# Routed experts behind a gated attention: where the first expert's weight steps stand, in which order two layers load, and where the last ranking stands

## The chip, the cores and the metric

The kernel runs on one core of a Trainium2 chip. The metric is the device time of one execution in microseconds; 0.5% of it is about 5 us. PE is the matmul engine (TensorE), ACT ScalarE, DVE VectorE, POOL GpSimd, SP the engine that issues most loads. [...]

## What is computed

```python
for t in range(S):                       # gated attention, 4 x 8 heads, 768 steps, head size 48
    state = alpha[:, :, t, :, None] * state + einsum('bhd,bhe->bhde', k[:, :, t], v[:, :, t])
    y[:, :, t] = einsum('bhd,bhde->bhe', q[:, :, t], state)
x = y as (3072, 384)
x = ((x @ w1) * (x @ w2)) @ w3 @ w_out   # dense gated layer, inner width 1024
logits = x @ w_gate + log1p(exp(x @ w_noise)) * noise      # 8 experts
top2, weights = the two largest of each token, their softmax
for e in range(8):                       # routed experts, 384 -> 1024 -> 384
    h = maximum(x[mask] @ ew1[e], 0)
    out[mask] += weight[mask] * (h @ ew2[e])
```

## The kernel before

**Three stages.** The attention and the dense layer are interleaved by a planner (L1150 to L1190): PE's order is written out by the program, the other engines' order is made by a scheduler when the kernel is built. Tokens go in eight groups g of 384. A group's dense layer is 16 wide units (`wide`, L523: for each of eight slices f and two matrices i, nine matmuls of 384 columns; ACT takes the result out as ab, DVE multiplies the two, L540, and splits the product into gh and gl, L181 and L183) and six narrow units (`narrow`, L546: twelve matmuls of 400 columns; three tiles t, two parts each). With the last narrow unit `finish` (L566) and `route` (L604) follow: some fifty small steps on DVE that end with the sums over R and the counts M (L645 to L648).

**Ranking.** `rank(g)` (L651) adds up the counts by two small matmuls (L657, L658), works out each token's row on DVE (L660 to L683, the rows are ad) and writes six lots into a table in device memory from POOL (L686). Group g-1 is ranked amid group g's wide units, behind slice RF in the last group. The first expert's part 0 needs the ranking of groups 0 to 6: SP then loads its slots mt from the table (L946), POOL gathers the tokens' rows xg (L887), and PE turns them (`turn_part`, L895) between the last narrow units. The last group's ranking, `rank(NG - 1)`, is called in `experts` among the first expert's tiles.

**An expert.** Part 0 has 512 slots, part 1 has 320. Layer 1 is eight units (`first`, L972, nine matmuls each: L902 to L904), whose result ACT splits off as hh (L905) and DVE as hl (L906). Layer 2 is a tile of 24 matmuls (`second`, L912 to L914), scaled by the factors wv (L951, from mt and the two scales) into ysb and added to the output by an indirect write from POOL (L936). Expert 0 and expert 1 are opened together: part 0 of expert 0, part 0 of expert 1, then the two parts 1.

**Weight steps.** Each layer's weights are loaded in halves into es (three tiles, L855), then cut into eh and el. `weight_steps` (L842) lists the steps: two loads, two maxima over a half (L858; the second also writes em, L861), an empty step, a small matmul of em on PE (`over_all`, L866), the scales on DVE (L870 to L874), then the cuts (ACT writes eh, L181, DVE writes el, L185). They wait in the list `todo`, and `prepare(n)` (L1014) takes n of them, each set behind the last DVE and ACT instruction of the program so far. A load takes a free es tile, so the fourth load waits for the cuts of the first half. In the list, layer 1's steps stand ahead of layer 2's. Before the change the first expert's steps begin behind the last group's ranking of group 6, one after each further wide and narrow unit (`prepare_after`); `leave(n)` in `experts` takes steps until n are left.

Of the kernel before, what the change touches and what calls it, by code (L numbers as in the profile page):

```python
# [24 lines left out]
E = 8  # L25
NK = DM // P
# [4 lines left out]
NG = NTOK // G  # L31
# [7 lines left out]
EST = P * TCOLS  # L39
NTA = G0 // P  # L40
NFR = 2
RF = 3
RG = 6
PA = 1
WB = 12
# [12 lines left out]
Q2 = 3  # L58
Q3 = 1
Q4 = 1  # L60
ST1 = 13
ST2 = 11
T0 = 1
T1 = 2
PGL = range(4)
NPC = 4
PB = 512
# [18 lines left out]
def body(ctx, tc, q, k, v, alpha, mw1, mw2, mw3, mwo, wg, wn, noise, ew1, ew2, out, dbg=None):  # L86
# [710 lines left out]
    def mix_units():  # L797
        fu = fuse_units()
        for g in range(NG):
            for f in range(NF):  # L800
                for i in range(2):
                    if g == 0:
                        yield (0.0, (lambda f=f: convert((f // 4 + 1) * 2 * NK + AH)), TG - 1)
                    yield (1.48, (lambda g=g, f=f, i=i: wide(g, f, i)), (g + 1) * TG - 1)
                    if g == NG - 1 and f > RF:
                        yield (0.0, (lambda: prepare_after(LAST[-1], PA)), 0)
                    if g == 0 and f >= FF:
                        c, x, n = next(fu)
                        yield 0.0, (lambda n=n: convert(n + AH)), 0
                        yield c, x, 0  # L810
                if f == (RF if g == NG - 1 else RG) and g:
                    yield (0.1, (lambda g=g: LAST.append(rank(g - 1))), 0)
                    if g == NG - 1:
                        yield (0.0, begin_experts, 0)
            if g == 0:
                for c, x, n in fu:
                    yield 0.0, (lambda n=n: convert(n + AH)), 0
                    yield c, x, 0
                yield (0.0, end_of_weights, 0)
            for t in range(TG):  # L820
                for part in range(2):
                    yield (2.05, (lambda g=g, t=t, part=part: narrow(g, t, part)), 0)
                    if g == NG - 1:
                        yield (0.0, (lambda: prepare_after(LAST[-1], PA)), 0)
                        if 0 <= t * 2 + part - T0 < NTP[0]:
                            yield (0.34, (lambda i=t * 2 + part - T0: turn_part(0, 0, i)), 0)

# [3 lines left out]
    def expert_weights(e):  # L831

        r, steps = [], []
        for j, (src, n, m) in enumerate(((ew1, NK, F), (ew2, NF, DM))):
            sc = ep.tile([P, 8], F32, name=f"esc{j}")
            hi = ep.tile([P, n, m], F16, name=f"eh{j}")
            lo = ep.tile([P, n, m], F16, name=f"el{j}")
            r += [hi, lo, sc]
            steps += weight_steps(src, e, n, m, hi, lo, sc)
        return r, steps  # L840

    def weight_steps(src, e, n, m, hi, lo, sc):  # L842

# [89 lines left out]
    def put(py, n, mt, wv, t, e=None):  # L933
        ys = ep.tile([P, DM], F32, name="ysb", bufs=3)
        nc.scalar.activation(ys[:n], py, AF.Copy, scale=wv[:n, t:t + 1])  # L935
        i = nc.gpsimd.indirect_dma_start(  # L936
            out=out, out_offset=bass.IndirectOffsetOnAxis(ap=mt[:n, t, 0:1].bitcast(U32), axis=0),
            in_=ys[:n], in_offset=None, compute_op=OP.add)
        if e == E - 1:
            for o in adds.setdefault(e, []):  # L940
                tc.declare_no_dep(i.ins, o.ins, reason="an expert has each token once")
            adds[e].append(i)
# [17 lines left out]
    def fetch_part(e, p):  # L960
        c0, c1 = PARTS[p]
        t0, nt = c0 // P, -(-(c1 - c0) // P)
        rows = P + NTOK - (G if e < NFR and p == 0 else 0)
        mt = slots(table[e, :, t0:t0 + nt, :], nt, p)
        xT = ep.tile([P, 2 * NK, nt * P], F16, name=f"xT{p}", bufs=1)
        EX[e, p] = (mt, xT, [gather(mt, t, rows) for t in range(nt)])
# [30 lines left out]

        return rest

    def begin_experts():  # L1000
        nonlocal ep
        ep = ctx.enter_context(tc.tile_pool(name="ep", bufs=2, side="right", reuse_waits="tile"))
        weights_for(0)
        fetch_part(0, 0)

    def weights_for(e):
        EW[e], st = expert_weights(e)
        todo.extend(st)

    def prepare_after(ins, n):  # L1010
        with tc.issue_after(ins):
            prepare(n)

    def prepare(n):  # L1014

        if not n or not todo:
            return
        with ExitStack() as st:
            for e in (mybir.EngineType.DVE, mybir.EngineType.Activation):
                for i in [i for i in nc.cur_bb.bb.instructions[-60:] if i.engine == e][-1:]:  # L1020
                    st.enter_context(tc.issue_after(i))
            for _ in range(min(n, len(todo))):
                todo.pop(0)()
# [4 lines left out]
    def experts():  # L1028
        leave(ST2)
        weights_for(1)  # L1030
        fetch_part(1, 0)
        for f in range(NF):
            first(0, 0, f)
            prepare(Q1)
        leave(ST1 + ST2)
        for t in range(NTP[0]):
            turn_part(1, 0, t)
            second(0, 0, t)
            prepare(Q2)
            if t == 1:  # L1040
                rank(NG - 1)
        fetch_part(0, 1)
        fetch_part(1, 1)
        leave(ST2)
        for f in range(NF):
            first(1, 0, f)
            prepare(Q3)
            if 0 <= f - NF + NTP[1] + T1 < NTP[1]:
                turn_part(0, 1, f - NF + NTP[1] + T1)
        for f in range(NF):  # L1050
            first(0, 1, f)
            prepare(Q4)
        leave(0)
        weights_for(2)
        for t in range(NTP[1] - 1):
            turn_part(1, 1, t)
            second(0, 1, t)
            prepare(2)
        turn_part(1, 1, NTP[1] - 1)
        rest = last_few(0)  # L1060
        prepare(2)
        li = overflow_plan()
        for e in range(1, E):
            if 1 < e < E - 1:
                weights_for(e + 1)
            if e > 1:
                fetch_part(e, 1)
                for f in range(NF):
                    first(e, 0, f)
                    if f == 0:  # L1070
                        rest()
                    prepare(1)
                    if 3 <= f < 3 + NTP[1]:
                        turn_part(e, 1, f - 3)
            if e + 1 < E:
                fetch_part(e + 1, 0)
            for f in range(NF):
                first(e, 1, f)
                if f == 0 and e == 1:
                    rest()  # L1080
                prepare(1)
            for t in range(NTP[0]):
                second(e, 0, t)
                prepare(2)
                if e + 1 < E:
                    turn_part(e + 1, 0, t)
            prepare(len(todo))
            if e < E - 1:
                for t in range(NTP[1] - 1):
                    second(e, 1, t)  # L1090
                rest = last_few(e)
        second(E - 1, 1, 0)
        rest = last_few(E - 1)
        second(E - 1, 1, 1, rest)
        return li
# [66 lines left out]
    load(0)  # L1162
    with tc.manual_schedule(engines={mybir.EngineType.PE}):
        M = iter(mix_units())
        nxt = next(M)
        ta = tm = t0 = 0.0
        warm(WB)
        for c, f in att_units():
            turned = set(done)
            f()  # L1170
            ready |= turned
            ta += c
            if MS not in done:
                t0 = ta
                dve = [i for i in nc.cur_bb.bb.instructions[-40:] if i.engine == mybir.EngineType.DVE]
                marks += dve[-1:]
                if marks:
                    with tc.issue_after(marks[max(0, len(marks) - LAG)]):
                        convert(int(CR * (ta - CS)))
                if c and 0 in done and nconv >= 2 * NK and pieces:  # L1180
                    wide(0, *pieces.pop(0), P)
                elif c:
                    warm(WP if ta < 4.1 else WU)
                continue
            while nxt is not None and nxt[2] in ready | {0} and tm < RATIO * (min(ta, TK) - t0) + R2 * max(ta - TK, 0.0) and nxt[1] is not begin_experts:
                nxt[1]()
                tm += nxt[0]
                nxt = next(M, None)
        att.close()
        while nxt is not None:  # L1190
            nxt[1]()
            nxt = next(M, None)
        li = experts()
    overflow(li)
# [32 lines left out]
```

## Time and profile before

| | us |
|---|---|
| three runs: lowest, median, highest | 997.57, 999.78, 1002.41 |
| profiled execution: its own time | 1000.15 |
| profiled execution: span from first to last instruction | 998.2 |
| mean granted clock | 0.973 |

The profiled execution lies 0.37 us above the median. All times below are microseconds from the start of its span. The attention's last product ends at about 486, the last group's wide units run from 506.63 to about 534, its narrow units and the first turns to 547.39, and the experts from there to the end.

How to read a row of the engines: start, duration, engine, line, operation, what it writes and reads, count; in brackets the idle time ahead of it and what ended it. Matmuls overlap, so a unit's price is the step from start to start.

### The profile page before, as it was taken

The numbers are of one execution on the slowest core, as the hardware profiler recorded it, in microseconds if no ns is written. First come the engines' busy times: TensorE is split into PE (matmuls) and PEld (weight loads), VectorE is DVE, ScalarE is ACT, GpSimd is POOL, SyncE is SP. The second block draws the span as 40 slices with busy tenths as digits, with TensorE's granted clock in tenths as the row PEclk, the third lists the DMA queues.
The fourth block names the chain that finished last, engine by engine and source line by source line (L and its number), as shares of the span: only waits on it lengthen the run. The fifth ranks groups of instructions, "written<-read, shape, count | busy, mean of one in ns | idle before, by whom it ended". The sixth has DMA issues, their size and how long they took to land. (4 is left out here: it accounts for less than half of the span.)

```text
span 998.2 us, 18279 instructions
## 1 busy us (share of the span) xinstructions
PE 943.4 (95%) x7159; PEld 624.8 (63%) x7159; DVE 615.6 (62%) x1696; ACT 496.9 (50%) x972; POOL 253.8 (25%) x246
## 2 busy tenths in 40 slices
PE   7889999999899998999999879999999999999996
PEld 4777677777566665767555346765656565656564
DVE  6698878676689696886555838527263544535220
ACT  3876665363545656555445435445353544444421
POOL 2121110004030403022215062342342424342313
PEclk9799899999999999999999989999999999999998
DMA  9895581507615033001103245444353454453303
GB/s 248 216 163 101 154 211 33 95 15 211 115 21 93 9 73 48 25 1 56 65 25 105 87 109 153 108 100 135 64 141 87 107 127 93 105 129 71 36 11 45
DMA packets 144472, 94.58 MB, mean 95 GB/s; under 512 B 112112, under 2 KB 130112, under 8 KB 144384
## 3 DMA queue, kind: packets, MB, share of 16 engines
q1 hardware_dynamic: 127824, 57.02, 24.4%
q0 software_dynamic: 16560, 36.37, 16.3%
q8 instruction: 57, 0.93, 0.4%
q14 instruction: 31, 0.25, 0.1%
HBM read 73.06 MB, written 20.31 MB: 94 GB/s over the span
## 5 line engine op out<-in xcount | busy, mean ns | idle before, releaser
L936 POOL DMA_INDIRECT out_dram<-ysb,mt x56 | 90.3, 1613 | 256.6 <-ACT ysb L935 137.8
L906 DVE SCALAR_TENSOR_TENSOR hl<-ps,hh 128x512 f16<-128x512 f32 (+1 forms) x128 | 74.3, 585 | 107.0 <-ACT hh L905 107.0
L904 PE MATMUL ps<-xT,el 128*128 128x320 f16 (+1 forms) x384 | 131.5, 342 | 5.1 <-DVE el L185 5.1
L902 PE MATMUL ps<-xT,eh 128*128 128x320 f16 (+1 forms) x384 | 131.5, 342 | 0.0
L903 PE MATMUL ps<-xT,eh 128*128 128x320 f16 (+1 forms) x384 | 131.3, 342 | 0.0
L913 PE MATMUL ps<-el,hh 128*128 128x384 f16 x384 | 125.8, 328 | 2.5 <-DVE el L185 2.5
L914 PE MATMUL ps<-eh,hl 128*128 128x384 f16 x384 | 125.8, 328 | 0.0
L912 PE MATMUL ps<-eh,hh 128*128 128x384 f16 x384 | 125.8, 328 | 0.0
L905 ACT ACTIVATE hh<-ps 128x512 f16<-128x512 f32 (+1 forms) x128 | 66.0, 516 | 105.5 <-PE ps L904 98.5
L935 ACT ACTIVATE ysb<-ps,wv 128x384 f32<-128x384 f32 (+1 forms) x56 | 32.4, 578 | 132.9 <-PE ps L914 71.0
L185 DVE SCALAR_TENSOR_TENSOR el<-es,esc,eh 128x512 f16<-128x512 f32 (+1 forms) x80 | 66.7, 855 | 48.8 <-ACT eh L181 47.2
L686 POOL DMA_INDIRECT table<-md,ad x48 | 48.3, 1005 | 142.3 <-DVE ad L683 126.0
L536 ACT ACTIVATE ab<-ps 128x384 f32<-128x384 f32 (+2 forms) x136 | 61.4, 466 | 21.1 <-PE ps L534 19.8
L183 POOL TENSOR_TENSOR sm<-sf,sm 128x512 f16<-128x512 f32 x24 | 27.9, 1183 | 164.5 <-ACT sm L181 164.5
L887 POOL DMA_INDIRECT xg<-x2s,mt x56 | 55.7, 995 | 50.5 <-PE ps L904 23.1
L532 PE MATMUL ps<-xT,w1h 128*128 128x384 f16 (+2 forms) x204 | 66.6, 327 | 2.0 <-ACT ab L536 1.6
L532 PE MATMUL ps<-xT,w0h 128*128 128x384 f16 (+2 forms) x204 | 65.7, 323 | 1.1 <-ACT xT L403 1.1
L181 ACT ACTIVATE gh<-ab 128x384 f16<-128x384 f32 (+2 forms) x68 | 34.4, 507 | 64.3 <-DVE ab L540 63.9
L533 PE MATMUL ps<-xT,w1h 128*128 128x384 f16 (+2 forms) x204 | 66.4, 326 | 0.0
L534 PE MATMUL ps<-xT,w1l 128*128 128x384 f16 (+2 forms) x204 | 66.3, 326 | 0.0
L556 PE MATMUL ps<-Wh,gh 128*128 128x400 f16 x192 | 63.9, 333 | 2.2 <-ACT gh L181 2.2
L534 PE MATMUL ps<-xT,w0l 128*128 128x384 f16 (+2 forms) x204 | 65.9, 324 | 0.0
(288 smaller groups left out, 2201.6 us busy)
## 6 DMA issues: line engine op xcount, KB each, us to landing
es<-in_moe_w_dram SPq DMA_DIRECT2D x32, 768.0 KB, 4.6
s<-in_moe_w_dram POOLq DMA_DIRECT2D x16, 512.0 KB, 4.2
out_dram<-zero POOLq DMA_DIRECT2D x5, 960.0 KB, 11.6
v<-in_v_dram SPq DMA_DIRECT2D x24, 192.0 KB, 3.1
x2s<-xr SPq DMA_DIRECT2D x24, 192.0 KB, 1.9
pad<-in_alpha_dram SPq DMA_DIRECT2D x21, 192.0 KB, 4.2
pad<-in_q_dram SPq DMA_DIRECT2D x21, 192.0 KB, 4.4
pad<-in_k_dram SPq DMA_DIRECT2D x21, 192.0 KB, 5.0
```

Of the source, the lines that this page charges most:

```text
L185: nc.vector.scalar_tensor_tensor(lo, src, scale, hi, op0=OP.mult, op1=OP.subtract)
L532: nc.tensor.matmul(pm, wab[i][0][:, kk, fs], xT[:, kk, cs], start=kk == 0, stop=False)
L533: nc.tensor.matmul(pm, wab[i][0][:, kk, fs], xT[:, NK + kk, cs], start=False, stop=False)
L534: nc.tensor.matmul(pm, wab[i][1][:, kk, fs], xT[:, kk, cs], start=False, stop=kk == NK - 1)
L902: nc.tensor.matmul(pm, w1h[:, kk, fs], xT[:, kk, :n], start=kk == 0, stop=False)
L903: nc.tensor.matmul(pm, w1h[:, kk, fs], xT[:, NK + kk, :n], start=False, stop=False)
L904: nc.tensor.matmul(pm, w1l[:, kk, fs], xT[:, kk, :n], start=False, stop=kk == NK - 1)
L906: nc.vector.scalar_tensor_tensor(hl[:, f], pm, 0.0, hh[:, f], op0=OP.max, op1=OP.subtract)
L912: nc.tensor.matmul(py[:n], hh[:, f, ts], w2h[:, f], start=f == 0, stop=False)
L913: nc.tensor.matmul(py[:n], hh[:, f, ts], w2l[:, f], start=False, stop=False)
L914: nc.tensor.matmul(py[:n], hl[:, f, ts], w2h[:, f], start=False, stop=f == NF - 1)
L936: i = nc.gpsimd.indirect_dma_start(out=out, out_offset=bass.IndirectOffsetOnAxis(ap=mt[:n, t, 0:1].bitcast(U32), axis=0), in_=ys[:n], in_o ...
```

## The change

- `open_experts`: the experts' pool is opened and the first expert's steps are put into `todo` when the attention's pools close, and one step is taken (PA = 1) after each unit with a cost from there on: the last narrow units of group 6, the last group's wide units, its narrow units. `begin_experts`, at its old call behind the ranking of group 6, only fetches part 0.
- RF from 3 to 4: in the last group the ranking of group 6 stands one slice later.
- The two layers' steps are merged: layer 2's first load stands behind layer 1's two loads, its second load ahead of layer 1's last three cuts.
- ST1 and ST2: how many steps `leave` leaves at two places; T1: the turns of expert 0's part 1 stand one unit later.
- `rank(NG - 1)` behind tile 0 of expert 0, not behind tile 1.
- Expert 0's writes to the output are declared independent of one another, as expert 7's already are.

```diff
-RF = 3
+RF = 4
-ST1 = 13
-ST2 = 11
+ST1 = 15
+ST2 = 9
-T1 = 2
+T1 = 1
...
-                    if g == NG - 1 and f > RF:
-                        yield (0.0, (lambda: prepare_after(LAST[-1], PA)), 0)
...
-                        yield (0.0, (lambda: prepare_after(LAST[-1], PA)), 0)
...
-            steps += weight_steps(src, e, n, m, hi, lo, sc)
-        return r, steps
+            steps.append(weight_steps(src, e, n, m, hi, lo, sc))
+
+        a, b = steps
+        return r, a[:2] + b[:1] + a[2:-NK] + b[1:2] + a[-NK:] + b[2:]
...
-        if e == E - 1:
+        if e in (0, E - 1):
             for o in adds.setdefault(e, []):
                 tc.declare_no_dep(i.ins, o.ins, reason="an expert has each token once")
...
-    def begin_experts():
+    def open_experts():
         nonlocal ep
         ep = ctx.enter_context(tc.tile_pool(name="ep", bufs=2, side="right", reuse_waits="tile"))
         weights_for(0)
+
+    def begin_experts():
         fetch_part(0, 0)
...
-            if t == 1:
+            if t == 0:
                 rank(NG - 1)
...
         att.close()
+        open_experts()
         while nxt is not None:
             nxt[1]()
+            if nxt[0]:
+                prepare(PA)
             nxt = next(M, None)
```

Lines of the changed kernel are up to three lower than those of before from there on (L865 there is L866 here).

PE at the end of the second wide unit of the last group (w1h and w1l are the second matrix's weights, w0h the first's, M and rb belong to the ranking). Before:

```order
L533 LDWEIGHTS w1h
L533 MATMUL ps<-xT,w1h 128x384
L534 LDWEIGHTS w1l
L534 MATMUL ps<-xT,w1l 128x384
L532 LDWEIGHTS w0h
L532 MATMUL ps<-xT,w0h 128x384
```

After:

```order
L533 LDWEIGHTS w1h
L533 MATMUL ps<-xT,w1h 128x384
L534 LDWEIGHTS w1l
L534 MATMUL ps<-xT,w1l 128x384
L865 LDWEIGHTS part
L865 MATMUL ps<-em,part 128x1
L532 LDWEIGHTS w0h
L532 MATMUL ps<-xT,w0h 128x384
```

The first expert's scale matmul, which in before stands behind wide unit 14, now stands behind wide unit 2.

DVE where the routing of group 6 ends (R, M and md are its last results; esc and em are the maxima of the first expert's weights). Before:

```order
L648 TENSOR_TENSOR R<-R,M 128x8
L183 TENSOR_TENSOR gl<-ab_6762,gh 128x384
L647 CAST M<-R 128x8
L642 COPY md<-ids 128x6
L648 TENSOR_TENSOR R<-R,M 128x8
L663 CAST rb<-R 128x8
L647 CAST M<-R 128x8
L660 COPY rk<-ps 128x24
```

After:

```order
L647 CAST M<-R 128x8
L642 COPY md<-ids 128x6
L648 TENSOR_TENSOR R<-R,M 128x8
L647 CAST M<-R 128x8
L648 TENSOR_TENSOR R<-R,M 128x8
L857 TENSOR_REDUCE esc_6544<-es 128x1
L663 CAST rb<-R 128x8
L647 CAST M<-R 128x8
L860 TENSOR_REDUCE em<-esc_6544 128x1
L869 COPY esc_6544<-ps 128x1
```

The second maximum of layer 1 and em now stand right behind the routing, ahead of the ranking's rk; the first maximum stands ahead of the routing.

DVE behind the ranking of the last group, in the first expert's layer 2 (wv_7814 are the factors of expert 0's part 1, el_7207 and el_7228 are expert 1's). Before:

```order
L683 TENSOR_TENSOR ad<-rs,rr 128x6
L870 COPY esc_7205<-ps 128x1
L871 TENSOR_SCALAR esc_7205<-esc_7205 128x1
L872 TENSOR_SCALAR esc_7205<-esc_7205 128x1
L873 TENSOR_SCALAR esc_7205<-esc_7205 128x1
L874 TENSOR_SCALAR esc_7205<-esc_7205 128x1
L185 SCALAR_TENSOR_TENSOR el_7207<-es,esc_7205,eh_7206 128x512 x2
L951 TENSOR_SCALAR wv_7814<-mt_7537,esc_6843,esc_6846 128x3
L185 SCALAR_TENSOR_TENSOR el_7207<-es,esc_7205,eh_7206 128x512 x4
```

After:

```order
L683 TENSOR_TENSOR ad<-rs,rr 128x6
L185 SCALAR_TENSOR_TENSOR el_7228<-es,esc_7226,eh_7227 128x512 x2
L857 TENSOR_REDUCE esc_7229<-es 128x1 x2
L185 SCALAR_TENSOR_TENSOR el_7228<-es,esc_7226,eh_7227 128x512
L860 TENSOR_REDUCE em<-esc_7229 128x1
L950 TENSOR_SCALAR wv_7814<-mt_7554,esc_6544,esc_6547 128x3
```

All of expert 1's el now stand ahead of the factors wv; in before four of the six stand behind them.

## Rows read from the trace of the kernel before

**Rows 1.** The page, its first part: busy time of an engine, share, instructions.
```profile
PE 943.4 (95%) x7159; PEld 624.8 (63%) x7159; DVE 615.6 (62%) x1696; ACT 496.9 (50%) x972; POOL 253.8 (25%) x246
```

**Rows 2.** Stages: length, busy time by engine (instructions), granted clock, DMA share, GB/s.
```profile
500.00:550.00 50.00, 46.83 (x298) 27.47 (x296) 27.62 (x105) 25.58 (x58) 14.87 (x16) 1.00 0.24 73
550.00:600.00 50.00, 40.76 (x212) 20.12 (x211) 30.35 (x97) 18.62 (x30) 16.61 (x14) 0.90 0.36 96
```

**Rows 3.** PE's waits, 460 to 600 us: total, times, longest.
```profile
PE ps L904 <- DVE el L185: 5.1, 1, 5.1
PE ps L866 <- DVE em L861: 3.5, 2, 1.9
PE ps L913 <- DVE el L185: 2.5, 2, 2.1
```

**Rows 4.** PE's instructions in order of time.
```profile
506.63 0.33 PE L532 MATMUL ps<-xT,w0h 128*128 128x384 f16 x1
...
509.55 0.33 PE L532 MATMUL ps<-xT,w0h 128*128 128x384 f16 x1
...
519.58 0.17 PE L658 MATMUL ps<-M,ones 128*128 128x24 bf16 x1 [0.99 <-DVE M L647]
...
530.91 0.18 PE L866 MATMUL ps<-em,part 128*128 128x1 bf16 x1 [1.94 <-DVE em L861]
...
537.93 0.50 PE L895 MATMUL ps<-ident,xg 128*128 128x128 f16 x6
...
547.39 0.38 PE L902 MATMUL ps<-xT,eh 128*128 128x512 f16 x1
...
569.03 0.48 PE L913 MATMUL ps<-el,hh 128*128 128x384 f16 x1 [2.13 <-DVE el L185]
...
571.86 0.33 PE L913 MATMUL ps<-el,hh 128*128 128x384 f16 x1
...
593.14 0.61 PE L904 MATMUL ps<-xT,el 128*128 128x512 f16 x1 [5.10 <-DVE el L185]
...
599.09 0.42 PE L903 MATMUL ps<-xT,eh 128*128 128x512 f16 x1
...
609.01 0.38 PE L902 MATMUL ps<-xT,eh 128*128 128x512 f16 x1
...
610.95 0.30 PE L902 MATMUL ps<-xT,eh 128*128 128x320 f16 x1
```

**Rows 5.** SP's loads of expert weights, in order of time.
```profile
470.22 15.03 SPq L855 DMA_DIRECT2D es<-in_moe_w_dram  x3
```

**Rows 6.** DVE's instructions in order of time.
```profile
507.50 0.17 DVE L176 TENSOR_SCALAR am<-am 128x3 int32<-128x3 int32 x1 [10.88 <-ACT xr L561]
...
518.90 0.55 DVE L183 TENSOR_TENSOR gl<-ab,gh 128x384 f16<-128x384 f32 x1
...
519.57 0.17 DVE L648 TENSOR_TENSOR R<-R,M 128x8 f32<-128x8 f32 x1
...
528.58 1.74 DVE L858 TENSOR_REDUCE esc<-es 128x1 f32<-128x1536 f32 x1
...
548.26 0.17 DVE L176 TENSOR_SCALAR am<-am 128x3 int32<-128x3 int32 x1 [1.73 <-ACT xr L561]
...
558.66 0.15 DVE L861 TENSOR_REDUCE em<-esc 128x1 bf16<-128x2 f32 x1
...
592.14 0.29 DVE L951 TENSOR_SCALAR wv<-mt,esc,esc 128x3 f32<-128x3 f32 x1 [7.59 <-DMA mt<-table]
592.34 2.73 DVE L185 SCALAR_TENSOR_TENSOR el<-es,esc,eh 128x512 f16<-128x512 f32 x4
```

**Rows 7.** POOL in order of time; last line: the gathers, 530 to 640 us.
```profile
522.84 0.96 POOL L686 DMA_INDIRECT table<-md,ad  x1 [21.33 <-DVE ad L683]
...
533.84 0.98 POOL L887 DMA_INDIRECT xg<-x2s,mt  x1 [3.72 <-DMA mt<-table]
...
DMA to landing us min/median/max: 3.0/3.1/6.4
```

More of the change, by code (lines that the diff above doesn't have):

```diff
@@ L1008, in weights_for @@
         todo.extend(st)
-    def prepare_after(ins, n):
-        with tc.issue_after(ins):
-            prepare(n)
     def prepare(n):
```

## Prediction

> **What bounds the kernel now.** I read the page first: PE is busy 95% of the span [rows 1], so a change is worth what it does to PE's idle time and to its stretches at the lower clock. The table by stages [rows 2] says where these are after the attention: from 550 to 600 us PE works 40.76 of 50 us at a mean granted clock of 0.90; from 500 to 550 it works 46.83 at 1.00. The list of PE's waits there [rows 3] names what this change touches: two waits of the scale matmuls for em (3.5 us), layer 2's wait for its el (2.5) and expert 1's first layer for its el (5.1); a fourth, the ranking's for the counts (0.99), stands in PE's own rows at 519.58 [rows 4].
>
> Those rows give the price of PE's work and the points I count from [rows 4]. Two wide units, 18 matmuls of 384 columns, take 506.63 to 509.55: 1.46 a unit, 0.1625 a matmul. A layer-2 tile has 24 of these, 3.9, and with a turn 4.24. Four turns and narrow units take 537.93 to 547.39, 9.46; a narrow unit (12 matmuls of 400) is 2.03 of it, a turn 0.34. A unit of layer 1 takes 609.01 to 610.95, 1.94. From expert 0's first unit (547.39) to the third pass of layer 1 (610.95) PE needs 63.56 us, but its work is 16 x 1.94 + 4 x 4.24 + 3 x 0.34 = 49.0. So **14.5 us** are lost there: 1.6 for em, 2.5 and 5.1 for el [rows 3], two stretches at 1.2 instead of 2.4 GHz, and a microsecond of small hops. The first stretch is 569.03 to 571.86, nine matmuls in 2.83 us instead of 1.47, 1.4 lost; the second 593.14 to 599.09, fourteen of layer 1 in 5.95 instead of 3.0, 3.0 lost [rows 4].
>
> **The early steps (weights begun at the attention's close).** The loads are no gain: before already issues three at 470.22 [rows 5]. The first maximum over es (L858, 1.74 us) can run in VectorE's idle 10.88 us ahead of 507.50 [rows 6], free. The second cannot: in the new order it stands behind the whole routing of group 6. That routing starts at 507.50, when the group's last narrow unit is evicted, an event that the change doesn't move, and in before its last sum over R is at 519.57. Of the six product pieces (L540, L183, 0.55 each) in between, four are gone; they partly filled gaps between dependent steps, so I take off 1.7, not 2.2: the routing ends at 517.9. Then 1.74 for the maximum, 0.16 for two casts and 0.2 from em to PE: the scale matmul starts at **520.0**. On PE it now stands behind the second wide unit, at 509.55. PE idles **10.4 us**, with wide units 3 to 16, the narrow units and the turns queued behind it.
>
> That VectorE holds ready work behind a waiting instruction is in the trace: wv waits 7.59 us for its table rows, and the four el queued behind it start right after, at 592.34 [rows 6]. [...]
>
> [...] The nearest rows are 1.4 us lost after a wait of 2.13 and 3.0 after one of 5.10 [rows 4]; no row shows 10. I take **2.4**, nearer to the longer wait, and keep both ends.
>
> **The chain to the first gather.** RF = 4 puts the ranking of group 6 behind wide unit 10: 520.0 + 2.4 + 8 x 1.46 = 534.1, counts at 534.4. In before the first table write follows the counts' matmul by 3.26 us (519.58 [rows 4], 522.84 [rows 7]); now two more el (about 0.75 each) lie in that chain on VectorE, and I take 4.85: 539.25. From the first table write to the first gather it is 11.0 us (522.84 to 533.84), and a gather lands 3.1 later [rows 7]. So the first turn (537.93 in before) can start at 539.25 + 11.0 + 3.1 + 0.1 = **553.45**, 15.5 later.
>
> What lies beside that costs nothing more. Layer 2's two maxima stand behind the ranking on VectorE and end, with one product, at 542.8, so PE waits for em a second time, from 538.85 to 542.95. Then 3 wide and 2 narrow units (4.4 + 4.06) bring PE to the turn at 551.4; the factors (wv), which hold the last product back until the slots land, make it 552.7. Both are ahead of 553.45; with an earlier gather they would be next.
>
> **First expert's layers.** From the first turn to expert 0's first unit it is 9.46 us as before: 563.0. Its weights are cut by then, so the waits for its el and for its second em are gone. In their place expert 1's em stands behind unit 7 on PE and, on VectorE, behind most of group 7's routing with six hl and two maxima. In before such a chain took 548.26 to 558.66, with four hl and two maxima [rows 6]; 13 more small steps of 0.2 and two hl of 0.6 make 14.4 from the routing's start. PE reaches the matmul 12.7 after it: **1.75 us** of waiting.
>
> In layer 2 the ranking of group 7 comes one tile earlier, and the writes of expert 0 no longer wait for one another, so its table writes start behind the first tile's write and not the second's. Expert 1's el all stand ahead of wv now and are done some 2 us before PE asks: the 5.1 us and the 3.0 behind them don't come back. Before's 14.5 become 1.75.
>
> **Sum.** 15.5 + 1.75 - 14.5 = +2.75 us. To this I add one more stretch at 1.2 GHz, 1.4: three more waits are left (4.1, about 2 in pieces, 1.75), and of before's four in 500 to 600 us the clock fell after two, those of 2.13 and 5.10; none fell ahead of 550, after 1.94 [rows 2, 4]. So **+4.2 us**. The profiled execution took 1000.15 us, 0.37 above the median of 999.78: 1004.3 against itself, **1003.9** as a median. The later experts keep their order but for em's matmul one unit later, where PE has no wait now; the end is untouched.
>
> **Rivals.**
> - Slower still: the clock falls after each wait. Place: PE at 520, 543, 553 and 577. Price: 3.0 instead of 2.4 first, then 1.0 (3.0, of which 2 hide before the gather), 1.4 and 1.4: 2.75 + 0.6 + 3.8 = +7.2, so 1007. It decides as soon as a second of the later waits lowers the clock. For it: two in four did. Against: the first of these falls may hide behind the gather.
> - Milder: no further fall, 1.4 instead of 2.4, the ranking's chain in 3.26: 2.75 - 1.0 - 1.6 = 0, so 1000. If table, slots and gather came in time altogether, the turn would start at 547.3 and the sum be -3.4, 996.4; against that, their 14.1 us [rows 7] alone reach past it.
> - Faster: em doesn't stand behind the routing in fact, and the change does what it is for. Then 10.4 and 2.4 go, the ranking is some 3 us late against before, and the sum is near -10, 990. Against it stand the order and the row of wv.
> - A new wait in expert 1's first pass: VectorE holds hl behind wv and the next expert's maximum, whose load is issued behind the slots on SP. I work out 6 us of lag, three units of the eight PSUM tiles that the pool has; over 8 us PE would stop. Price up to the 5.1 that went, 1009.
>
> **Chances.** Forecast 0.50 (1002 to 1005.5), slower still 0.25, milder 0.15, faster 0.04, new wait 0.06. A measurement can tell about 0.5% (5 us: under 994.8, over 1004.8) from no change. Slower: 0.25 + 0.06 and a fifth of the forecast, 0.41. Faster: 0.04 and the lowest of milder, 0.06. Same: 0.53. The range 998 to 1009 leaves out the faster case, the low end of milder and the tops of the two slow ones, some 0.15.
>
> **What would show it.** PE must wait about 10 us for em behind the second wide unit and come back at 1.2 GHz; the first turn must start near 553, held by the gather or by gl; layer 2 and expert 1's first layer must have no wait for el; the third pass must start near 614 (610.95 now). If PE waits under 3 us at the first em, I have read VectorE's order wrongly, and with it the sign. If that wait is there but the third pass starts ahead of 609, the chain to the gather is what I got wrong.

## The result, and the profile after

The changed kernel takes 1006.76 us (median; 1003.69 to 1012.42), the kernel before 999.67 beside it: a ratio of 1.007, with an interval of 1.005 to 1.0089. A second measurement gave 1007.55 against 998.69, 1.0076 [1.0043, 1.0109]. The change costs 7 to 9 us. The forecast was 1003.9, 4.2 above before, and "within 0.5%" had the largest chance: the sign of the sum was right, and some 3 to 5 us of it were missing. The result lies inside the stated range (998 to 1009) and above the forecast's own band (up to 1005.5).

The profiled execution took 1006.21 us, with a span of 1004.5. The first part of its page (busy time of an engine, share, instructions) answers [rows 1]:

```profile
PE 942.4 (94%) x7159; PEld 625.5 (62%) x7159; DVE 617.1 (61%) x1696; ACT 497.8 (50%) x972; POOL 255.2 (25%) x246
```

PE does the same work in 6 us more. The stages (length, busy time by engine, granted clock, DMA share, GB/s) answer [rows 2]:

```profile
500.00:550.00 50.00, 35.70 (x194) 19.88 (x193) 30.47 (x107) 19.80 (x43) 7.50 (x8) 0.83 0.14 44
550.00:600.00 50.00, 47.03 (x291) 25.63 (x290) 29.84 (x95) 22.75 (x42) 17.92 (x17) 1.00 0.36 102
600.00:650.00 50.00, 47.07 (x376) 29.95 (x375) 28.56 (x64) 23.81 (x44) 17.17 (x17) 1.00 0.43 105
```

From 500 to 550 PE lost 11.1 us of work and the mean granted clock fell to 0.83, from 550 to 600 PE won 6.3, and from 600 to 650 it lost 2.9. In before it had not idled at all in that last stretch:

```profile
600.00:650.00 50.00, 50.00 (x409) 32.89 (x408) 33.47 (x68) 24.16 (x44) 15.55 (x15) 1.00 0.48 126
```

PE's longest waits from 480 to 640 us (total, times, longest) answer [rows 3]:

```profile
PE ps L865 <- DVE em L860: 15.9, 3, 10.7
...
PE ps L901 <- DVE el L185: 1.1, 1, 1.1
```

The waits of 5.1 and 2.5 us for el are gone (one of 1.1 is left), and one em wait of 10.7 us has come. VectorE's rows (start, duration, line, result; idle time ahead in brackets) answer [rows 6] and show where it comes from:

```profile
493.91 1.74 DVE L857 TENSOR_REDUCE esc<-es 128x1 f32<-128x1536 f32 x1
504.87 0.17 DVE L176 TENSOR_SCALAR am<-am 128x3 int32<-128x3 int32 x1 [9.22 <-ACT xr L561]
...
515.70 0.17 DVE L648 TENSOR_TENSOR R<-R,M 128x8 f32<-128x8 f32 x1
515.78 1.75 DVE L857 TENSOR_REDUCE esc<-es 128x1 f32<-128x1536 f32 x1
517.58 0.15 DVE L860 TENSOR_REDUCE em<-esc 128x1 bf16<-128x2 f32 x1
```

The first maximum is free, in VectorE's idle time ahead of the routing; the second, of the same weights, waits for no load, but starts only behind the routing's last sum. PE's and POOL's rows answer [rows 4, 7]:

```profile
517.79 0.16 PE L865 MATMUL ps<-em,part 128*128 128x1 bf16 x1 [10.71 <-DVE em L860]
...
532.43 0.17 PE L658 MATMUL ps<-M,ones 128*128 128x24 bf16 x1
...
540.62 0.18 PE L865 MATMUL ps<-em,part 128*128 128x1 bf16 x1 [3.60 <-DVE em L860]
...
551.68 0.51 PE L894 MATMUL ps<-ident,xg 128*128 128x128 f16 x6 [0.74 <-DMA xg<-x2s,mt]
...
616.12 0.30 PE L901 MATMUL ps<-xT,eh 128*128 128x320 f16 x1 [0.58 <-ACT xT L895]
```

```profile
536.98 0.96 POOL L686 DMA_INDIRECT table<-md,ad  x1 [38.08 <-DVE ad L683]
...
547.96 1.49 POOL L886 DMA_INDIRECT xg<-x2s,mt  x1 [3.69 <-DMA mt<-table]
```

The last group's first wide unit starts at 506.63 in the first trace of before and between 501.3 and 506.6 in all traces of this study, whatever the kernel: the attention ahead of it varies. So I count from that unit. The table gives PE's start of four points, in us behind it, from PE's rows in order of time: the first turn, expert 0's first unit of layer 1, expert 1's first unit, and the first turn of expert 1's part 1, which follows the third pass (expert 0's part 1). From that last point to the end of the span it is 377.4 to 377.9 us in every trace but e9's (382.1).

| kernel | first turn | expert 0 | expert 1 | behind the third pass | ratio to before |
|---|---|---|---|---|---|
| before | 31.3 | 40.8 | 79.3 | 114.1 | |
| before again (e7) | 31.3 | 40.8 | 78.0 | 111.6 | |
| forecast | 46.8 | 56.4 | 90.6 | 116.9 | |
| after | 47.7 | 58.2 | 92.5 | 122.6 | 1.007 |
| after again (e0) | 46.9 | 56.3 | 90.6 | 122.1 | |
| after again (e8) | 46.8 | 56.2 | 90.5 | 124.2 | 1.0076 |
| e1 both maxima ahead | 40.0 | 49.5 | 83.7 | 115.3 | 1.005 |
| e2 begin undone | 31.2 | 40.7 | 85.6 | 114.2 | 1.0023 |
| e3 = e1, RF = 3 | 36.4 | 45.8 | 80.1 | 111.7 | 1.001 |
| e4 = after, maxima behind hl | 46.7 | 56.1 | 90.4 | 116.8 | 1.006 |
| e5 = e3, cuts later | 33.7 | 45.2 | 79.7 | 111.9 | 1.0026 |
| e6 all of these | 33.6 | 45.2 | 79.9 | 106.2 | 0.9952 |
| e9 = before, rank and writes alone | 31.3 | 42.9 | 81.7 | 109.1 | 0.9944 |
| e10 = e6, em later | 33.8 | 44.6 | 82.2 | 109.0 | 0.9934 |
| e11 = e9, maxima behind hl | 31.3 | 40.8 | 78.0 | 105.5 | 0.9935 |

(The forecast's row is its own instants less 506.63; expert 1's first unit follows from its prices, 8 x 1.94 + 4 x 4.24 + 1.75 behind expert 0's, and the last is 107.1 for the third pass's start and 9.8 for the pass, as in before. The 1.4 that it added for one more slow stretch is not in the row.)

Each ratio is to the kernel before timed beside that run. The median of before was between 996.16 and 999.67 us in these groups, so a ratio says more than a time.

The table already says where the forecast failed. Up to expert 1's first unit it agrees with e0 and e8 within 0.2 us; the first trace of the changed kernel is 0.9 to 1.9 later. What it had not was behind that: from expert 1's first unit to the last point the changed kernel needs 30.1, 31.5 and 33.7 us, and 26.3 was forecast.

### The profile page after: what moved, and what is told of

Its sections match the earlier page's. It is cut to its first block, busy times and chain, and to the rows that moved or that the text cites. A ratio compares the mean times of both kernels' runs of the same rounds, so it can differ in the third digit from the quotient of the medians.

```text
span 1004.5 us, 18279 instructions
## 1 busy us (share of the span) xinstructions
PE 942.4 (94%) x7159; PEld 625.5 (62%) x7159; DVE 617.1 (61%) x1696; ACT 497.8 (50%) x972; POOL 255.2 (25%) x246
## 4 chain that ended last, share of the span: by engine, by line
PE 59%; DVE 18%; issue 9%; ACT 8%; DMA 3%; POOL 2%; SPq 1%; another core or an unknown queue 0%; POOLq 0%; ACTq 0%; DVEq 0%
PE ps L911 6%; PE ps L913 6%; PE ps L912 6%; PE ps L903 6%; PE ps L901 6%; PE ps L902 6%; PE ps L558 2%; PE ps L556 2%; PE ps L557 2%; PE ps L894 2%; PE ps L350 2%; DVE Gx L236 2%; DVE ab L540 1%; PE ps L300 1%; PE ps L532 1%
## 5 line engine op out<-in xcount | busy, mean ns | idle before, releaser
L935 POOL DMA_INDIRECT out_dram<-ysb,mt x56 | 90.6, 1617 | 246.2 <-ACT ysb L934 142.8
L901 PE MATMUL ps<-xT,eh 128*128 128x320 f16 (+1 forms) x384 | 130.1, 339 | 2.2 <-DVE el L185 1.1
L185 DVE SCALAR_TENSOR_TENSOR el<-es,esc,eh 128x512 f16<-128x512 f32 (+1 forms) x80 | 67.0, 854 | 44.9 <-ACT eh L181 42.9
L886 POOL DMA_INDIRECT xg<-x2s,mt x56 | 56.1, 1001 | 51.5 <-PE ps L903 19.1
L532 PE MATMUL ps<-xT,w0h 128*128 128x384 f16 (+2 forms) x204 | 66.0, 325 | 1.1 <-ACT xT L403 1.1
L533 PE MATMUL ps<-xT,w0h 128*128 128x384 f16 (+2 forms) x204 | 66.0, 325 | 0.0
```

What stands on the lines that cost most here:

```text
L532: nc.tensor.matmul(pm, wab[i][0][:, kk, fs], xT[:, kk, cs], start=kk == 0, stop=False)
L533: nc.tensor.matmul(pm, wab[i][0][:, kk, fs], xT[:, NK + kk, cs], start=False, stop=False)
L901: nc.tensor.matmul(pm, w1h[:, kk, fs], xT[:, kk, :n], start=kk == 0, stop=False)
L935: i = nc.gpsimd.indirect_dma_start(out=out, out_offset=bass.IndirectOffsetOnAxis(ap=mt[:n, t, 0:1].bitcast(U32), axis=0), in_=ys[:n], in_o ...
```

## The experiments

**The changed kernel again.**

> The changed kernel a second time, for a second trace of it. If its losses are made by the order of its instructions, this trace shows again 10 to 11 us of PE waiting for the first em behind the second wide unit, a first turn 13 to 17 us later than in the trace before, and 3 to 4 us of small PE waits between expert 1's first unit and the third pass, with hh (ScalarE) starting about 5 us behind the matmuls of its unit. If the last of these was an accident of one execution (PE's results reached ScalarE and VectorE late there, with no cause in the order), the third pass starts 3 us or more closer to expert 1's first unit here.

It took 1005.73 us. PE's waits from 480 to 640 us, then SP, VectorE and PE about the third pass:

```profile
PE ps L865 <- DVE em L860: 15.9, 3, 10.7
PE ps L901 <- DVE hl L905: 3.4, 1, 3.4
```

```profile
610.15 0.33 SPq L945 DMA_DIRECT2D mt<-table  x1
610.57 0.92 SPq L854 DMA_DIRECT2D es<-in_moe_w_dram  x2
```

```profile
608.66 0.68 DVE L905 SCALAR_TENSOR_TENSOR hl<-ps,hh 128x512 f16<-128x512 f32 x1
615.18 1.75 DVE L857 TENSOR_REDUCE esc<-es 128x1 f32<-128x1536 f32 x1 [4.91 <-DMA es<-in_moe_w_dram]
616.85 0.68 DVE L905 SCALAR_TENSOR_TENSOR hl<-ps,hh 128x512 f16<-128x512 f32 x1
```

```profile
617.59 0.42 PE L901 MATMUL ps<-xT,eh 128*128 128x320 f16 x1 [3.43 <-DVE hl L905]
...
626.50 0.50 PE L894 MATMUL ps<-ident,xg 128*128 128x128 f16 x6
```

The waits for em repeat to 0.05 us. The small waits ahead of the third pass do not, nor does ScalarE's lag there: they were of one execution. In their place stands one wait inside the third pass. VectorE has hl to make for the fifth unit of expert 1, but ahead of it in its order stands the maximum over half of expert 2's weights. Their load left SP at 610.57, behind the slots of the next part at 610.15, and landed near 615. That hl came at 616.85, 12.1 us behind its unit (595.0 + 5 x 1.94 = 604.7). The hl behind it were 9 to 10.5 us late, each holding a PSUM tile of the eight that the pool has, and PE stopped for 3.43 us and came back at half the clock (granted 0.68 in the mean from 616 to 620 us; its matmuls of 320 columns stand 0.27 us apart up to 620.74 and 0.135 behind that). The pass took 14.9 us instead of 9.8.

**What that costs.** A maximum can be put behind the last hl of the third pass, with its loads left where they are:

```diff
-            nc.vector.tensor_reduce(sc[:, 5 + i:6 + i], s[i], AX.XY, OP.max, apply_absolute_value=True)
+            with ExitStack() as st:
+                if isinstance(e, int) and e == 2:
+                    st.enter_context(tc.issue_after(HL[-1]))
+                nc.vector.tensor_reduce(sc[:, 5 + i:6 + i], s[i], AX.XY, OP.max, apply_absolute_value=True)
...
         nc.vector.scalar_tensor_tensor(hl[:, f], pm, 0.0, hh[:, f], op0=OP.max, op1=OP.subtract)
+        HL.append(nc.cur_bb.bb.instructions[-1])
...
+    HL = []
```

> The changed kernel with one thing more: the maxima over the third expert's (expert 2's) first layer are set behind the last hl of expert 0's part 1 on VectorE; its loads stay where they are. My theory (in expert 0's part 1 PE stops 3.4 us for hl, which stands on VectorE behind a maximum whose load came late, and comes back at the lower clock): that wait and the slow stretch are gone, 5.3 us between the first unit of expert 1 and expert 1's part 1, the rest as in the changed kernel: a ratio to the kernel before of about 1.002. Rival (the slots or the gathered rows of that part are as late and would stop PE in its place): 1.005 to 1.007.

VectorE at the end of the third pass of this kernel, then PE at expert 1's first unit and behind the third pass:

```profile
621.16 0.49 DVE L908 SCALAR_TENSOR_TENSOR hl<-ps,hh 128x320 f16<-128x320 f32 x1 [0.73 <-ACT hh L907]
621.57 3.40 DVE L860 TENSOR_REDUCE esc<-es 128x1 f32<-128x1536 f32 x2
```

```profile
594.17 0.38 PE L904 MATMUL ps<-xT,eh 128*128 128x512 f16 x1
...
620.49 0.50 PE L897 MATMUL ps<-ident,xg 128*128 128x128 f16 x6
```

In the trace the wait is gone, nothing took its place, and the stretch is 26.3 us, the forecast's own number; the span is 6.0 below e0's. The times show less: 999.91 us, a ratio of 1.006 [1.0038, 1.0081], where 1.002 was expected and the rival had 1.005 to 1.007, though its mechanism is not in the trace; the medians lie only 3.3 us apart. The loss in the stretch differs from execution to execution: 3.8, 5.2 and 7.4 us in three traces of the changed kernel. In the first of them the same hl was as late (it ended at 619.18, and PE goes on at 619.23), but PE, held up by small waits ahead of the pass, waited only 0.51 us for it:

```profile
619.23 0.30 PE L901 MATMUL ps<-xT,eh 128*128 128x320 f16 x1 [0.51 <-issue]
```

The intervals of the two ratios, 1.006 and 1.0076, overlap. So the cause of the wait is shown, its price as a median is not.

**The first em.** One step is taken as soon as the attention closes, so that both maxima stand ahead of the routing:

```diff
         open_experts()
+        prepare(1)
         while nxt is not None:
```

> One step of the first expert is taken at once when the attention closes, so that both maxima over es and em stand ahead of the routing of group 6 on VectorE; all else as in the changed kernel. My theory (the second maximum behind the routing costs 10.7 us of waiting and 2.9 us of slow clock): no PE wait for em behind the second wide unit, the ranking's matmul some 13 us earlier than in the changed kernel, the first turn near 537 to 540, the el waits still gone: 992 to 996 us, about 0.993 of the kernel before. Rival (the chain from the ranking to the gather, one slice later, sets the first turn and the em wait lay beside it): the first turn waits some 10 us for xg and the time stays at 1002 to 1007. Second rival (the loss is in expert 1's first pass and after): 1003 to 1006.

1001.15 us, 1.005 [1.0033, 1.0068]. The wait of 10.7 us is gone and the first turn stands 6.9 us earlier than in e0, not the 12 to 15 that were expected. PE's waits:

```profile
PE ps L865 <- DVE em L860: 5.2, 2, 3.6
PE ps L901 <- DVE hl L905: 3.6, 1, 3.6
...
PE ps L556 <- ACT gh L181: 1.3, 1, 1.3
```

The expectation had left a consequence of its own edit out: with em early, the scales and the el of 0.74 us come early too. Four of the six el stand amid the routing, whose end is on the path to the counts. Waits for the counts (0.9), for the second em (3.6 us again) and for gh (1.3), with their slow stretches (the mean granted clock is 0.90 from 500 to 550 us), took half of the gain. The wait in the third pass stayed.

> As e1_both_ahead, with RF = 3: the ranking of group 6 one slice earlier. If in e1_both_ahead the first turn waits for its gathered rows, this one is up to 2.9 us faster than that (two wide units of 1.46); if not, the two are the same within 1 us.

996.28 us, 1.001 [0.9996, 1.0023]: a slice earlier is worth 3.6 us at the first turn. That is more than either case of the expectation had: in e1 no turn waits for its gathered rows, and still the time fell; the waits that shrank are those for the second em (3.6 to 1.6 at most) and for gh. The rest is in the next kernel's target: in e3 the routing lasts from 504.75 to 519.93, 15.2 us, against 12.1 in e2, where no cut stands in it. The edit, against e3:

```diff
-                [lambda: None, over_all, scales] +
+                [lambda: None, over_all] + [lambda: None] * (7 if isinstance(e, int) and e == 0 and n == NK else 0) + [scales] +
```

> As e3_both_ahead_rf3, with seven empty steps ahead of the first expert's scales, so that its six cuts stand behind the ranking of group 6 on VectorE and not amid that group's routing. My theory (the six el of 0.75 us and the scales lengthen the routing by some 3 us, and PE waits for the counts, 4.9 us in three waits, and then runs at the lower clock for 3 us): the waits at the ranking fall to about 1 us, the slow stretch behind them goes, the first turn stands 5 to 8 us earlier against the last group's first wide unit: a ratio of 0.993 to 0.997. Rival (cuts so late make PE wait at layer 2 or at expert 1's em for them): 0.998 to 1.002.

997.83 us, 1.0026 [1.001, 1.0042], not faster, and above the rival's range too. The waits for the counts fell to 1.2 us as expected, the first turn stands 2.7 us earlier and not 5 to 8, and two other waits came:

```profile
PE ps L894 <- DMA xg<-x2s,mt: 4.4, 1, 4.4
PE ps L901 <- DVE em L860: 4.2, 1, 4.2
```

With the cuts late the es tiles come free late: SP issues two loads of weights at 533.08 and 534.11, between and behind the slots, and the first gather, issued at 535.29, lands only when PE turns at 540.2, 4.9 us later. The first gathers take 3.7 us to landing in the median there (531 to 541 us), and 3.0 in e2 (527 to 537), without such loads. That the loads made it late is argued from this pair and not shown. (The row for em at L901 stands in the third pass, at 609.65, where e0's names hl: the same wait, behind a maximum that waits 6.39 us for its load.)

**Which part gains.** The early part undone, all else kept:

```diff
-RF = 4
+RF = 3
...
+                    if g == NG - 1 and f > RF:
+                        yield (0.0, (lambda: prepare_after(LAST[-1], PA)), 0)
...
+                        yield (0.0, (lambda: prepare_after(LAST[-1], PA)), 0)
...
     def begin_experts():
+        open_experts()
         fetch_part(0, 0)
...
-        open_experts()
         while nxt is not None:
             nxt[1]()
-            if nxt[0]:
-                prepare(PA)
...
```

> The changed kernel with its early part undone: the experts' pool and the first expert's steps begin behind the ranking of group 6 again, RF is 3 again; the merged list, the counts left, T1, the ranking of the last group behind tile 0 and the unordered writes stay. My theory: the early part costs and the late part gains. The wait for expert 1's el (5.1 us) and the 3.0 us of slow clock behind it are gone, 1 to 4 us come back as a wait in expert 1's first pass: 993 to 998, some 10 us below the changed kernel. Rival (the late part brings nothing, since the slots come from the table no earlier or hl stands behind the next expert's maximum): 999 to 1003.

998.72 us, 1.0023 [1.0004, 1.0042]. The early part thus costs some 5 us of the changed kernel's 7 to 9, but the remainder does not gain: the ratio came out where the rival put it, for another reason. With the merged list begun late, the last two cuts of expert 0's layer 1 fall behind the routing of the last group, on both engines:

```profile
557.88 0.20 ACT L636 ACTIVATE w<-w 128x3 f32<-128x3 f32 x1 [5.67 <-DVE w L635]
557.99 1.32 ACT L181 ACTIVATE eh<-es,esc 128x512 f16<-128x512 f32 x2
```

```profile
558.75 0.61 PE L904 MATMUL ps<-xT,eh 128*128 128x512 f16 x1 [4.78 <-ACT eh L181]
```

So the ranking and the writes were tried alone, in the kernel before:

```diff
-        if e == E - 1:
+        if e in (0, E - 1):
             for o in adds.setdefault(e, []):
...
-            if t == 1:
+            if t == 0:
                 rank(NG - 1)
```

> The kernel before with two edits of the change alone: the ranking of the last group behind tile 0 and the unordered writes of expert 0. My theory (these bring the slots one tile earlier, so wv no longer holds up expert 1's el): the wait of 5 us for el in expert 1's first layer shrinks to 0 to 1.5 and the slow stretch of 3 us behind it goes: a ratio of 0.992 to 0.996. Rival (the el go only because the merged steps put them ahead of wv; the slots alone come too late): the wait stays over 3 us: 0.997 to 1.001.

994.4 us against 998.69, 0.9944 [0.9922, 0.9965]: faster than before and than the changed kernel. (The traced execution, 998.55 us, is the slowest of its ten.) The wait for el, 5.03 us in e7, is 0.79 in e9 and 0.76 in e11, whose expert 1 begins where e7's does (78.0 in both). VectorE and PE in e7, then in e11:

```profile
588.45 0.29 DVE L951 TENSOR_SCALAR wv<-mt,esc,esc 128x3 f32<-128x3 f32 x1 [7.51 <-DMA mt<-table]
```

```profile
589.45 0.61 PE L904 MATMUL ps<-xT,el 128*128 128x512 f16 x1 [5.03 <-DVE el L185]
```

```profile
582.45 0.29 DVE L955 TENSOR_SCALAR wv<-mt,esc,esc 128x3 f32<-128x3 f32 x1 [7.83 <-DMA mt<-table]
582.65 4.06 DVE L185 SCALAR_TENSOR_TENSOR el<-es,esc,eh 128x512 f16<-128x512 f32 x6
```

```profile
583.45 0.39 PE L907 MATMUL ps<-xT,el 128*128 128x512 f16 x1 [0.76 <-DVE el L185]
```

From the last group's first unit wv comes after 84.1 us in e7 (588.45 less 504.37) and after 78.3 in e11 (582.45 less 504.13): the slots are 5.8 us earlier, and that is the wait, though all six el still stand behind wv; no slow stretch follows it (from 583.68 to 590.83 PE does 33 matmuls of layer 1 at 0.217 us each, 1.95 a unit against the 1.94 of an undisturbed one). Which of the two edits brings the slots earlier was not tried. The next loss of e9, in VectorE's rows, is maxima ahead of hl again:

```profile
614.98 1.75 DVE L858 TENSOR_REDUCE esc<-es 128x1 f32<-128x1536 f32 x1 [2.72 <-DMA es<-in_moe_w_dram]
...
618.94 1.75 DVE L858 TENSOR_REDUCE esc<-es 128x1 f32<-128x1536 f32 x1 [1.35 <-DMA es<-in_moe_w_dram]
620.61 0.48 DVE L906 SCALAR_TENSOR_TENSOR hl<-ps,hh 128x320 f16<-128x320 f32 x1
```

PE waits 2.4 us for that last hl in layer 2. The edit of e4 on top, which sets the maxima behind hl here too:

> e9_rank_tile0 with the edit of e4_max_behind_hl: the maxima over expert 2's first layer behind the last hl of expert 0's part 1. In e9_rank_tile0 two of these maxima wait 2.7 and 1.4 us for their loads with hl queued behind them, PE waits 2.4 us for hl in expert 0's part 1 of layer 2 and its first two tiles take 6.8 and 5.9 us instead of 4.2. If that is the same mechanism, these 4.3 us go: a ratio of 0.989 to 0.992, at least as good as e6_all and e10_all_later with three edits. Rival (the loads themselves, or the gathered rows, hold that part up): 0.993 to 0.996, no change.

990.37 us against 996.9, 0.9935 [0.9905, 0.9965]. The wait for hl is gone from the trace, and its last point is the earliest of all (105.5). But the ratio lies in the rival's range, and the step from 0.9944 is not resolved.

**All repairs together.**

> e5_cuts_later with e4_max_behind_hl's edit, the turns of expert 0's part 0 one narrow unit later (T0 = 2) and one more empty step ahead of expert 1's em (its small matmul behind unit 8 and not unit 7). If the three losses are separate and as the traces say (5.3, 5 to 8, 1.5 us): 0.987 to 0.991. If removing one wait only uncovers the next (xg, wv, the es loads), it stays within 2 us of the better of e4_max_behind_hl and e5_cuts_later.

991.26 us against 996.6, 0.9952 [0.993, 0.9973]: some 5 us faster than before, about half of what a sum of separate losses gave, and more than the other case allowed. PE's waits:

```profile
PE ps L868 <- DVE em L863: 3.6, 2, 2.0
PE ps L904 <- ACT xT L898: 2.3, 1, 2.3
...
PE ps L897 <- DMA xg<-x2s,mt: 0.5, 1, 0.5
```

One more kernel sets the second em of expert 0 four steps later (five empty steps in its list in place of one; that line is not shown here) and takes more steps among the first units:

```diff
-            prepare(Q1)
+            prepare(2 if f < 3 else Q1)
...
-            prepare(Q2)
+            prepare(Q2 + (t == 0))
```

> e6_all with the first expert's second em four steps later, and three steps more taken among the first units and one behind tile 0. In e6_all PE waits 1.65 us for that em, 0.5 for xg, 2.3 for xT and 2.0 for expert 1's second em, and loses about 2 us at the lower clock. If these are separate: 4 to 7 us below e6_all, 0.988 to 0.991. If the gathered rows come next (e6_all already waits 0.5 for them): only 0 to 3 us below, 0.992 to 0.995.

991.94 us against 998.69, 0.9934 [0.991, 0.9958]: with the em wait gone the turn waits 2.4 us for its rows instead of 0.5, as the rival said, and layer 2 waits for its cuts (1.6 and 1.4). As a ratio the step from 0.9952 is not resolved.

**The two baselines.**

> The kernel before a second time, for a second trace of it: which of its losses repeat. The wait of 5.1 us for el in expert 1's first layer with 3.0 us of slow clock behind it should be there again, and 0 to 2 us less in the attention, where the changed kernel and its variants start the last group 1.6 to 3.8 us earlier than the first trace of before.

995.45 us. The wait for el is there again, 5.03 us, and the last group starts at 504.37, 2.3 us earlier, a little more than the 0 to 2 expected. The slow stretch behind layer 2's wait, 1.4 us in the first trace, is not (from expert 0's first unit to expert 1's it is 37.2 us and not 38.5, with the same wait of 2.1), nor is all of the other: the last point stands at 111.6 and not 114.1.

> The changed kernel again, timed beside the kernel before on the chip of the next two, since the two traces of before differ by 4.7 us. By the traces (from the last group's first wide unit to the second turn row of expert 1's part 1: 114.1 and 111.6 us in before, 122.6 and 122.1 in the changed kernel) it lies 8 to 10.5 us above before: a ratio of 1.008 to 1.011. If the first measurement (1.007) is the better one: 1.005 to 1.008.

1.0076, inside the range of the first measurement (1.005 to 1.008) and just under the one taken from the traces. Its trace has the wait in the third pass at 4.5 us.

## Why the prediction was right and wrong

**The first em: right.** 10.4 us were forecast, 10.71 and 10.69 came, for the reason given: the second maximum stands behind the routing. The clock's price, 2.4 from rows of other waits, was 2.8 in the first trace and 1.8 in e0's (two units from 518.17 to 522.89, 4.72 us, less 2 x 1.46).

**The chain to the first gather: right, its meeting with the first turn in part luck.** From the counts' matmul to the first table write 4.55 us (4.85 forecast), from there to the gather 10.98 (11.0), to the first turn 3.72 (3.2). The first turn stands 46.8 to 47.7 us behind the group's first unit; 46.8 was forecast. The second em wait was 3.60 to 3.65 (4.1), but it was not hidden as stated in every trace: a slow stretch of 1.7 to 2.8 us behind it, which the sum did not have, took up the rest of the cover. In the first trace the turn still waited 0.74 us for its rows. In e0 and e8 PE came to it (at 551.26 in e0) with no wait at all: there PE's own path, which the forecast had 0.75 to 2 us ahead of the gather, set the first turn. That both paths end close to one another, 0.74 us apart in the first trace, is why the instant came out.

**Expert 0's layers: right.** The third em wait was 1.55 (1.75), the waits for el in layer 2 and in expert 1's first layer are gone, and the third pass starts 107.2 us behind the group's first unit in e0 and 107.1 in e8, where 107.1 was forecast. The first trace has 112.1, behind the small waits and ScalarE's lag that did not come again. Before has 104.3 there in its first trace, +2.9 against a sum of +2.75, and 101.8 in its second, +5.3.

**The wait in the third pass: wrong.** It was the fourth rival, "VectorE holds hl behind wv and the next expert's maximum, whose load is issued behind the slots on SP", given 0.06. The mechanism was named, and weighed by one number, 6 us of lag against the 8 that it estimated the PSUM tiles to bear. The 6 is near for the maximum it was worked out for: in e0 expert 1's first hl starts 7.2 us behind its unit (604.09 against 596.9), and PE does not stop. The step that failed is that it looked at the first of the maxima only. The second half of the same layer stands four hl further on, its load leaves SP behind another load of slots, and those wait for a write to the output to land:

```profile
SPq L945 <- DMA out_dram<-ysb,mt: 13.6, 2, 6.8
```

(SP's waits in e0, 585 to 625 us.) The hl behind it started 12.1 us behind its unit. Not all of that is the slots': by the order in which the three es tiles come round, the tile for this load was free only at 607.2, behind the el that starts at 606.21, so waiting for the slots added some 3 us to the load's start at 610.57. Seen from the result, the second load would have made the rival worth some 5 us (3.8 to 7.4 were lost in the stretch) and the sum about +8. That VectorE holds work behind what stands ahead of it, which the prediction read from the row of wv, is what both waits show: the second maximum, which waits for no load, stood behind the routing, PE waited 10.69 us for its em, and e1, which sets it ahead, has no such wait; hl stood behind a maximum that it does not need and that waited 4.91 us for its load, PE waited 3.43 us for it, and e4, which changes that last order alone, has no such wait. Besides the stretch behind the first em the forecast added one more, 1.4. Two came: one behind the second em wait, nearly all under the gather's cover, and in e0 and e8 one behind this wait (mean granted clock 0.97 and 0.93 from 600 to 650 us). The prediction gives the clocks of these stretches in GHz, 1.2 instead of 2.4; no run shows a clock in GHz. The traces show a granted clock of 0.50 and of 1.00, and matmuls of 384 columns 0.320 us apart at the one (518.73 to 523.53 in the first trace of the changed kernel) and 0.163 at the other (544.28 to 546.72).

**Slower still: its number, not its mechanism.** That rival, given 0.25, stood at 1007, next to the 1006.76 measured. It let the clock fall behind each of the four waits, for 3.8 us besides the first. But the first turn came where the forecast without these falls had it, within 0.9 us, and behind the third em wait the clock did not fall (granted 1.00 from 576 to 580 us in the first trace, and from 550 to 600 in e0). The missing microseconds were lost behind that, in a wait that this rival does not have.

**Before's 14.5 us: too large by 2.5.** From expert 0's first unit to the third pass the second trace of before needs 61.07 us (545.13 to 606.20), the first 63.56: the slow stretch behind layer 2's wait, 1.4 us, was of one execution, and the other was shorter in the second. The sum took a loss that one of two traces has for a fixed one.

**What each part is worth.** The ranking behind tile 0 and the unordered writes alone are 0.9944 (e9). With the merged list, the counts and T1 on top it is 1.0023 (e2), and with the early start and RF = 4 besides 1.007: two parts of the change cost what its third gains, and more. The forecast put the gain for el down to two things, the earlier ranking and the el ahead of wv; e9 and e11 have it with all six el behind wv.

## What to carry to other kernels

A step that is set early helps only if its whole chain is early on every engine: here one unit of delay between two maxima put the second behind fifty small steps on VectorE, and PE waited 10.7 us for it. Where ready work stands behind an instruction that waits for a load, as hl did behind a maximum that waited 4.91 us, follow every such load through the queue that issues it, not the first alone: here hl was 7.2 us late at the first and 12.1 at the second. And a change made of several orders is worth taking apart: two of its lines gave 4 to 6 us that the other parts hid.

## What the runs showed of the hardware

The loss at the lower clock did not grow with the wait ahead of it here. In e0 the granted clock fell while PE idled, was 0.50 before the wait of 10.69 us ended, and was back at 1.00 from 522 us on:

```profile
510.00:514.00 4.00, 0.00 (x0) 0.00 (x0) 3.52 (x17) 0.31 (x1) 0.00 (x0) 0.70 0.15 51
514.00:518.00 4.00, 0.00 (x0) 0.00 (x0) 3.81 (x22) 0.21 (x1) 0.00 (x0) 0.50 0.00 0
518.00:522.00 4.00, 3.86 (x14) 1.89 (x14) 0.77 (x7) 0.49 (x1) 0.00 (x0) 0.52 0.00 0
522.00:526.00 4.00, 4.00 (x27) 2.39 (x26) 1.74 (x3) 2.28 (x5) 0.00 (x0) 1.00 0.00 0
```

1.8 us were lost behind it, 2.8 behind the wait of 3.65 us (three units from 540.0 to 547.2 instead of 4.4), and none behind the third (granted 1.00 from 550 to 600). In the first trace of the changed kernel it was 2.8 behind 10.71, 1.7 behind 3.60 and none behind 1.55 (granted 1.00 from 576 to 580). Nor did a wait of one length cost the same each time: behind layer 2's wait, 2.13 us in the first trace of before and 2.1 in the second, the first lost 1.4 us, the second none.

In the first trace of the changed kernel ScalarE saw a unit's end late: the last matmul of expert 1's first unit starts at 598.22, and its hh starts at 604.03 (in e0 at 597.15, for a unit that ends near 596.9). No row says what held it up, and it came in none of the other traces to this extent; it stays open.

```profile
598.22 0.38 PE L903 MATMUL ps<-xT,el 128*128 128x512 f16 x1
```

```profile
604.03 0.60 ACT L904 ACTIVATE hh<-ps 128x512 f16<-128x512 f32 x1 [2.31 <-remote]
```
